# Attention and MLP on one core: where k and q of the last six quads of heads are transposed

## The chip, the core and the metric

One core of one Trainium2 chip runs the whole program. The metric is device time in microseconds (us), the median of several runs. Five engines work side by side and meet at semaphores: TensorE (PE; PEld is its weight load), VectorE (DVE), ScalarE (ACT), GpSimd (POOL) and SyncE (SP). SP and POOL also issue DMAs, each in the order of its own queue.

## The reference

Batch 8, 8 heads, 576 tokens, head depth 64, all float32. Attention with a decay by a gate f, then an MLP over the 4608 tokens by 512 features:

```
scores = q @ k.T / 8 + cum[:, None] - cum[None, :]     # cum: running sum of log f; causal
attn   = softmax(scores) @ v                           # per batch and head
x      = attn, heads side by side                      # 4608 x 512
out    = gelu_tanh(x @ w_in) @ w_out                   # 512 -> 2048 -> 512
```

## The kernel before

The work is cut twice. A **quad** is four heads of one batch: 16 quads, quad i belonging to batch i // 2. A **chunk** is 512 tokens of the MLP: 9 chunks. The MLP of a chunk runs between the quads' attention, so that TensorE always has something to do while other engines work on exponentials and sums. The MLP uses products of block sums (seven products in place of eight, L586 and L509).

The order of everything is written out by hand in tables of words (L71 to L110): FRONT, then SECOND for chunk 2, STEADY for chunks 3 to 5, FLUSH for chunk 6, LAST for chunk 7. Each word is a call (the table `ops`, L754), for example S.3.0: scores of quad 3, round 0. Numbers of quads are shifted by twice the chunk, those of chunks and batches by the chunk: S.4.0 in chunk 4 is quad 12, LB.2.0 loads values of batch 6. Every engine runs its share of the words in this order, and waits where it needs another's result.

The words around the change:

- LK, LQ (`load_one`, L206): one GpSimd DMA each loads k or q of a quad, cast to bfloat16, into k_c or q_c (two buffers each, by i % 2): head h on partitions 32h to 32h+31, 18 tokens to a partition.
- TK, TQ (`transpose_words`, L212): VectorE transposes 32x32 blocks of 4-byte words, each word two neighbouring depths in bfloat16, into kT or qT [128, tokens, 2]. Head h then has its depth on 32 partitions, as two halves c = 0, 1. kT has 64 zero tokens at either end.
- S (`scores`, L259): a quad's causal scores, in 3 rounds of 512 columns (the lists `pieces` and `rounds`). A round has, for each half c, each piece and each head, one matmul with 32 rows of depth and 128 keys; the four heads lie in four row tiles and write four PSUM banks in two tiles ps_s. Then two exponentials of ScalarE (L285), one for each pair of heads.
- M (L287): GpSimd zeroes the corners above the diagonal. VW (L227): GpSimd scales the values. D, V (L356, L374): denominators and outputs, matmuls of L347 on 32-column tiles; VectorE writes the attention's output into xT (L379). CL: a small copy.
- LB (L181): five loads of v for the batch after next, on SP's queue. Q, I, i: first layer of the MLP. T: VectorE's sums of x. G: its sums of gelus. F, f: second layer (L600), whose finished corners VectorE adds (L617 to L624) and SP stores (L625), from three buffers o_st. X, Y: ScalarE loads its table of exponentials or of gelus.

In STEADY the chunk begins with two loads (LK.4, LQ.4); LK.5 and LQ.5 follow; the four transposes TQ.3, TK.3, TK.4, TQ.4 stand in the MLP's first layer, ahead of G.0 and S.3.0. FLUSH has the last two, TK.3 and TQ.3.

Of the kernel before, what the change touches and what calls it, by code (L numbers as in the profile page):

```python
# [8 lines left out]
FP32 = mybir.dt.float32  # L9
BF16 = mybir.dt.bfloat16  # L10
AF = mybir.ActivationFunctionType
# [5 lines left out]
def kernel(  # L17
# [10 lines left out]
    nc = tc.nc  # L28

    B, H, S, D = q.shape  # L30
    BH = B * H
    NT = (S + 127) // 128
    LAST = S - 128 * (NT - 1)
    SPAD = NT * 128
    scale = 1.0 / (D ** 0.5)
# [6 lines left out]
    QPB = H // 4  # L42
# [7 lines left out]
    rounds = [(0, 512), (512, 512), (1024, 512)]  # L50
    pieces = [
        ("low", 0, 0, 64),
        (0, 64, 64, 512),
        (1, 576, 128, 448),
        (2, 1024, 256, 320),
        (3, 1344, 384, 192),
        ("high", 0, 512, 64),
    ]
    QA = 256
    split_rounds = [(1152, 384), (0, 512), (512, 320), (832, 384)]  # L60
    split_pieces = [
# [26 lines left out]
    SECOND = """  # L88
        Y F.-1.99 T.0.1 T.0.2 LB.2.0 T.0.3 T.0.4 LB.2.1 I.0.0 LB.2.2 E.0.2.2 I.0.1 LB.2.3 TK.3 LK.5 LB.2.4 E.0.2.2 TQ.3 LQ.5 TQ.4 I.0.2 E.0.2.2 I.0.3
        E.0.2.1 TK.4 G.0 VW.3 I.0.6 I.0.7 G.1.1.2 X F.0.13 S.3.0 M.3.0 f.0.9 UW.0.1 D.2 f.0.9 S.3.1 M.3.1 V.2.0 f.0.12 S.3.2 M.3.2 CL.3 V.2.1 VW.4  # L90
        f.0.14 S.4.0 UW.0.2 M.4.0 D.3 f.0.10 V.3.0 UW.0.4 CL.4 UW.0.3 S.4.1 f.0.13 M.4.1 V.3.1 S.4.2 F.0.9 M.4.2 F.0.2 F.0.1
    """

    STEADY = """
        LK.4 LQ.4 Q.0.2 Y LB.2.0 T.0.1 T.0.2 LB.2.1 F.-1.2 Q.0.2 i.0.2.4 T.0.4 LB.2.2 i.0.2.4 T.0.3 Q.0.2 TQ.3 LQ.5 Q.0.2 F.-1.6 i.0.3.4 Q.0.2 Q.0.2
        LB.2.3 TK.3 LB.2.4 LK.5 i.0.3.4 Q.0.2 TK.4 TQ.4 F.-1.99 I.0.6 i.0.7 G.0 S.3.0 X G.1.1.2 f.0.16 M.3.0 D.2 VW.3 f.0.12 S.3.1 M.3.1 V.2.0 f.0.13
        S.3.2 M.3.2 CL.3 V.2.1 VW.4 f.0.15 S.4.0 D.3 f.0.10 V.3.0 M.4.0 CL.4 S.4.1 f.0.14 M.4.1 V.3.1 S.4.2 F.0.12 M.4.2
    """

    FLUSH = """  # L100
        T.0.3 TK.3 F.-1.2 Y Q.0.2 T.0.1 T.0.2 Q.0.2 i.0.2.4 T.0.4 i.0.2.4 Q.0.2 Q.0.2 TQ.3 F.-1.6 i.0.3.4 Q.0.2 Q.0.2 i.0.3.4 Q.0.2 F.-1.99 I.0.6 i.0.7
        G.0 F.0.19 X S.3.0 G.1.1.2 D.2 f.0.11 M.3.0 f.0.4 S.3.1 M.3.1 V.2.0 VW.3 f.0.20 S.3.2 V.2.1 CL.3 M.3.2 f.0.21 f.0.12 D.3 f.0.15 V.3.0 v.3.1
    """

    LAST = """
# [6 lines left out]
    singles = ctx.enter_context(tc.tile_pool(name="singles", bufs=1))  # L112
# [4 lines left out]
    psS = ctx.enter_context(tc.tile_pool(name="psS", bufs=2, space=bass.MemoryType.PSUM))  # L117
# [3 lines left out]
    def many(n, shape, dtype, name):  # L121
        return [singles.tile(shape, dtype, name=f"{name}{i}") for i in range(n)]
# [2 lines left out]
    utri_f32 = singles.tile([128, 128], FP32, name="utri_f32")  # L125
    ones_f32 = singles.tile([128, 128], FP32, name="ones_f32")

    q_c = many(2, [128, S // 32, D], BF16, "q_c")
    k_c = many(2, [128, S // 32, D], BF16, "k_c")
    v_nat = many(2, [128, NT, H, D], FP32, "v_nat")  # L130
    qT = many(2, [128, S, 2], BF16, "qT")
    kT = many(2, [128, S + 128, 2], BF16, "kT")

    vw = many(2, [128, NT + 1, 4, D], BF16, "vw")
    pt = many(2, [128, 4, 3 * 512], BF16, "pt")
    RING = 4 * S
    xT = singles.tile([128, N_DT, RING], BF16, name="xT")
# [74 lines left out]
    def transpose_words(src, dst):  # L212
# [5 lines left out]
                .rearrange("p (a d) -> p a d", d=D // 2),  # L218
        )

    def transpose_k(i):
        return transpose_words(k_c[i % 2], kT[i % 2][:, 64:64 + S])

# [29 lines left out]
    def keep_busy(n, cols=512):  # L253

        for _ in range(n):
            nc.tensor.matmul(idle_ps[0][:, 0:cols], idle[:, 0:128], idle[:, 0:cols],
                             start=True, stop=True)

    def scores(i, r, groups=((0, 1, 2, 3),)):  # L259

        qq, p = qT[i % 2], pt[i % 2]
        if i < 2:
            off, n = split_rounds[r]
            todo = [(key, col - off, q0, nq) for (key, col, q0, nq) in split_pieces[r]]
        else:
            off, n = rounds[r]
            todo = []
            for (key, col, q0, nq) in pieces:
                a, z = max(col, off), min(col + nq, off + n)
                if a < z:  # L270
                    todo.append((key, a - off, q0 + a - col, z - a))
        for heads in groups:
            tiles = {g: psS.tile([128, 2, 512], FP32, name="ps_s", tag="s") for g in sorted({h // 2 for h in heads})}
            for c in range(2):
                for j, (key, c0, q0, nq) in enumerate(todo):
                    for h in heads:
                        nc.tensor.matmul(  # L277
                            tiles[h // 2][:, h % 2, c0:c0 + nq],
                            key_columns(i, key, h, c),
                            qq[32 * h:32 * h + 32, q0:q0 + nq, c],  # L280
                            start=(c == 0 and j == 0), stop=(c == 1),
                            skip_group_check=True,
                        )
            for g, t in tiles.items():
                nc.scalar.activation(p[:, 2 * g:2 * g + 2, off:off + n], t[:, :, 0:n], AF.Exp, scale=scale)  # L285
# [39 lines left out]
    def product(i, groups, spare, part=None):  # L325
        p = pt[i % 2]
        if part is not None:
            s0, s1 = parts[part]
            po = psM.tile([128, 512], FP32, name="po_m", tag="m")
            for (key, col, q0, nq) in sorted(sum(split_pieces[1:] if part else split_pieces[:1], []), key=lambda x: HIGH if x[0] == "high" else x[0]):  # L330
                for (r0, lhsT, h) in groups:
                    w = lhsT(HIGH if key == "high" else key)
                    nc.tensor.matmul(
                        po[r0:r0 + w.shape[-1], q0 - s0:q0 - s0 + nq], w, p[:, h, col:col + nq],
                        start=(key == 0), stop=(key == (HIGH if part else 1)),
                        skip_group_check=True,
                    )
            return po[:, 0:s1 - s0]
        if spare:
            po = psS.tile([128, 2, 512], FP32, name="ps_o", tag="s").rearrange("p a n -> p (a n)")  # L340
        else:
            po = psO.tile([128, 1024], FP32, name="po", tag="po")
        for (key, col, q0, nq) in sorted(pieces, key=lambda x: {0: 0, "low": 1}.get(x[0], 2)):
            t = {"low": LOW, "high": HIGH}.get(key, key)
            for (r0, lhsT, h) in groups:
                w = lhsT(t)
                nc.tensor.matmul(  # L347
                    po[r0:r0 + w.shape[-1], 448 + q0:448 + q0 + nq], w, p[:, h, col:col + nq],
                    start=(key in (0, "low")), stop=(key in ("low", "high")),
                    skip_group_check=True,  # L350
                )
        return po[:, 448:448 + S]

    rbs = {}

    def denominators(i, part=None):  # L356

        def column(h):

            return lambda t: (w_bf[:, i, t, h:h + 1] if t not in (0, LOW) else  # L360
                              w_bf[:, i, t, h:h + 1].to_broadcast([128, 32]))

        po = product(i, [(32 * h, column(h), h) for h in range(4)], False, part)
        n = S if part is None else parts[part][1] - parts[part][0]
        den = den_pool.tile([128, S], FP32, name="den", tag="den")
        nc.vector.transpose(out=den[:, 0:n], in_=po)
        rec = den_pool.tile([128, S // 32], FP32, name="rec", tag="rec")
        nc.vector.reciprocal(rec[:, 0:n // 32], den[:, 0:n:32])
        rb = den_pool.tile([128, S], FP32, name="rb", tag="rb")
        nc.vector.transpose(out=rb[:, 0:n].rearrange("p (c j) -> p c j", j=32),  # L370
                            in_=rec[:, 0:n // 32].unsqueeze(2).to_broadcast([128, n // 32, 32]))
        rbs[i, part] = rb[:, 0:n]

    def attn_out(i, x, spare=False, part=None):  # L374
        b, u = i // QPB, i % QPB
        po = product(i, [(32 * h, lambda t, h=h: vw[i % 2][:, t, h, x:D:2], h) for h in range(4)], spare, part)
        s0, s1 = (0, S) if part is None else parts[part]
        r0 = S * b % RING
        nc.vector.tensor_mul(xT[:, 2 * u + x, r0 + s0:r0 + s1], po, rbs[i, part])  # L379
# [371 lines left out]
    def load_values(b, half):  # L751
# [11 lines left out]
        "M": lambda i, r, *keys: mask(i, r, keys),  # L763
        "m": lambda i, r, *keys: mask_by_product(i, r, keys),
        "D": denominators,
        "V": lambda i, x, *part: attn_out(i, x, False, *part),
        "v": lambda i, x, *part: attn_out(i, x, True, *part),
        "VW": lambda i, *part: make_vw(i, nc.gpsimd, *part),
# [33 lines left out]
        "Y": load_gelu,  # L802
    }

    per_quad, per_chunk = ("S", "M", "D", "V", "v", "VW", "CL", "TK", "TQ", "LK", "LQ"), ("F", "f", "I", "i", "Q", "LB", "E", "e", "T", "t")

    def run(table, c=0):

# [15 lines left out]
    with tc.manual_schedule():  # L824
        setup()
        run(FRONT)
        for c in range(2, NCH):
            run(SECOND if c == 2 else STEADY if c < B - 2 else FLUSH if c == B - 2 else LAST if c == B - 1 else "", c)


# [28 lines left out]
```

## Time and profile before

| | |
|---|---|
| three runs | 324.68, 326.06, 326.25 us; median 326.06 |
| span of the profiled execution | 324.3 us |
| TensorE clock granted | full, in all 40 slices |
| chunk 3, 4, 5 (S.4.2 to S.4.2) | 33.6 us each: 134.0, 167.6, 201.2, 234.8 |
| score matmuls (L277) | 896, 36.3 us busy |
| VectorE's transposes of k and q (L214) | 32, mean 1.25 us |
| GpSimd's loads of k and q (L208) | 32 |

The profile shows one execution. A group's row has its line, engine, operation, shapes and count, then busy time and the mean of one in ns, then the idle time just before and what ended it. The chain of work that ended last goes back from the last instruction, at each step to what released it. Rows of stages give busy time by engine in a window, then the clock, the DMA engines' share and GB/s. TensorE's matmuls are pipelined: the distance from one group's start to the next's says more than a matmul's own length. The profile gives no time of its own for the profiled execution besides its span.

### The profile page before, as it was taken

The numbers are of one execution on the slowest core, as the hardware profiler recorded it, in microseconds if no ns is written. First come the engines' busy times: TensorE is split into PE (matmuls) and PEld (weight loads), VectorE is DVE, ScalarE is ACT, GpSimd is POOL, SyncE is SP. The second block draws the span as 40 slices with busy tenths as digits, with TensorE's granted clock in tenths as the row PEclk, the third lists the DMA queues.
The fourth block names the chain that finished last, engine by engine and source line by source line (L and its number), as shares of the span: only waits on it lengthen the run. The fifth ranks groups of instructions, "written<-read, shape, count | busy, mean of one in ns | idle before, by whom it ended". The sixth has DMA issues, their size and how long they took to land.

```text
span 324.3 us, 11816 instructions
## 1 busy us (share of the span) xinstructions
PE 310.0 (96%) x5337; PEld 221.2 (68%) x5337; DVE 241.7 (75%) x374; ACT 212.6 (66%) x242; POOL 107.0 (33%) x145
## 2 busy tenths in 40 slices
PE   0799989999999999999999999999999999999996
PEld 0557844454677667776788877767776786788785
DVE  3664307998989978779876998599885866597574
ACT  4495667686766786678667876877587743846610
POOL 8868507253111405510752056305610150000000
PEclk9999999999999999999999999999999999999999
DMA  6999999577034951395119610981001011010202
GB/s 117 232 155 165 196 250 217 139 160 143 8 67 88 227 116 36 76 213 107 36 40 211 143 40 6 206 183 35 7 32 67 17 35 53 16 50 2 99 33 98
DMA packets 47490, 33.41 MB, mean 103 GB/s; under 512 B 29776, under 2 KB 42192, under 8 KB 47440
## 3 DMA queue, kind: packets, MB, share of 16 engines
q0 software_dynamic: 9632, 15.99, 28.4%
q1 hardware_dynamic: 37664, 16.60, 18.9%
q8 instruction: 41, 0.67, 0.8%
q14 instruction: 9, 0.07, 0.1%
q10 hardware_dynamic: 144, 0.07, 0.1%
HBM read 36.85 MB, written 9.44 MB: 143 GB/s over the span
## 4 chain that ended last, share of the span: by engine, by line
PE 82%; DMA 6%; POOL 4%; ACT 4%; DVE 2%; issue 1%; POOLq 0%; DVEq 0%
PE ps_w L600 30%; PE ps_h L395 19%; PE po L347 9%; PE ps_q L520 8%; PE ps_s L277 8%; DMA w_out_sb<-in_moe_w_out_dram 4%; PE ps_u L468 4%; PE pso L667 4%; DMA q_c<-in_q_dram 2%; ACT pt L285 2%; POOL pt L291 1%; POOL w_out_sb L201 1%; POOL v_nat L185 1%; POOL w_in_sb L197 1%; PE cum_ps L721 1%
## 5 line engine op out<-in xcount | busy, mean ns | idle before, releaser
L285 ACT ACTIVATE pt<-ps_s 128x1024 bf16<-128x1024 f32 (+2 forms) x100 | 93.9, 990 | 41.3 <-PE ps_s L277 37.1
L291 POOL TENSOR_SCALAR_AFFINE_SELECT pt<-pt 128x512 bf16<-128x512 bf16 (+3 forms) x65 | 40.8, 639 | 98.0 <-ACT pt L285 75.2
L395 PE MATMUL ps_h<-xT,w_in_sb 128*128 128x512 bf16 (+1 forms) x320 | 66.8, 358 | 0.3 <-ACT gT L403 0.2
L395 PEld LDWEIGHTS <-w_in_sb 128*128 128x128 bf16 x320 | 31.2, 98 | 26.7 <-issue 0.6
L600 PEld LDWEIGHTS <-gT 128*32 128x32 bf16 (+1 forms) x1216 | 44.2, 97 | 5.5 <-issue 2.2
L403 ACT ACTIVATE gT<-ps_h 128x1024 bf16<-128x1024 f32 x34 | 34.6, 1017 | 18.7 <-PE ps_h L395 18.4
L600 PE MATMUL ps_w<-w_out_sb,gT 128*32 128x256 bf16 (+1 forms) x1008 | 42.6, 273 | 0.0
L277 PE MATMUL ps_s<-qT,kT 32*128 32x64 bf16 (+5 forms) x896 | 36.3, 263 | 4.6 <-DVE qT L214 4.3
L600 PEld LDWEIGHTS <-gsum 128*32 128x32 bf16 (+1 forms) x948 | 35.5, 97 | 3.6 <-issue 1.3
L231 POOL TENSOR_TENSOR vw<-v_nat,wT 128x1280 bf16<-128x1280 f32 (+1 forms) x13 | 29.6, 2278 | 11.8 <-DMA v_nat<-in_v_dram 11.5
L536 DVE TENSOR_TENSOR usnap<-ps_q,usnap 128x1024 f32<-128x1024 f32 x15 | 17.9, 1222 | 18.6 <-PE ps_q L520 13.2
L277 PEld LDWEIGHTS <-kT 32*128 32x128 bf16 x896 | 16.5, 93 | 20.9 <-issue 11.5
L600 PE MATMUL ps_w<-usum,gsum 128*32 128x256 bf16 (+1 forms) x791 | 29.9, 273 | 0.0
L617 DVE COPY snap<-ps_w 128x512 f32<-128x512 f32 x32 | 21.8, 681 | 6.1 <-PE ps_w L600 6.0
L531 ACT ACTIVATE gT<-usnap 128x1024 bf16<-128x1024 f32 x15 | 15.8, 1054 | 12.1 <-DVE usnap L536 11.8
L379 DVE TENSOR_TENSOR xT<-po,rb 128x576 bf16<-128x576 f32 x26 | 19.5, 752 | 5.6 <-PE po L347 5.3
L347 PE MATMUL po<-pt,vw 128*32 128x64 bf16 (+4 forms) x624 | 22.4, 278 | 0.0
L214 DVE STREAM_TRANSPOSE qT<-q_c 128x576 f32<-128x576 f32 x16 | 19.8, 1247 | 2.7 <-DMA q_c<-in_q_dram 2.5
L214 DVE STREAM_TRANSPOSE kT<-k_c 128x576 f32<-128x576 f32 x16 | 19.5, 1248 | 3.1 <-DMA k_c<-in_k_dram 3.1
L347 PEld LDWEIGHTS <-vw 128*32 128x32 bf16 x672 | 14.8, 97 | 9.3 <-issue 2.8
L208 POOL DMA_DIRECT2D k_c<-in_k_dram x16 | 9.1, 569 | 33.7 <-DVE kT L214 17.4
L520 PEld LDWEIGHTS <-w_in_sb 128*128 128x128 bf16 x160 | 15.6, 98 | 2.5 <-issue 0.4
(134 smaller groups left out, 478.4 us busy)
## 6 DMA issues: line engine op xcount, KB each, us to landing
out_dram<-o_st SPq DMA_DIRECT2D x35, 256.0 KB, 2.3
k_c<-in_k_dram POOLq DMA_DIRECT2D x16, 288.0 KB, 5.2
q_c<-in_q_dram POOLq DMA_DIRECT2D x16, 288.0 KB, 6.2
v_nat<-in_v_dram SPq DMA_DIRECT2D x16, 256.0 KB, 5.3
v_nat<-in_v_dram SPq DMA_DIRECT2D x20, 128.0 KB, 4.9
v_nat<-in_v_dram POOLq DMA_DIRECT2D x8, 256.0 KB, 8.2
w_in_sb<-in_moe_w_in_dram POOLq DMA_DIRECT2D x8, 256.0 KB, 7.6
w_out_sb<-in_moe_w_out_dram POOLq DMA_DIRECT2D x4, 512.0 KB, 11.1
```

The lines of the kernel that those rows point to most:

```text
L214: return nc.vector.transpose(out=dst.rearrange("p s c -> p (s c)").bitcast(FP32) .rearrange("p (t a) -> p a t", a=S // 32), in_=src.rearra ...
L231: return eng.tensor_mul(vw[i % 2][:, t0:t1], vb[:, t0:t1, h0:h0 + 4, :], wT[:, i, t0:t1, :].unsqueeze(3).to_broadcast([128, t1 - t0, 4, D]))
L277: nc.tensor.matmul(tiles[h // 2][:, h % 2, c0:c0 + nq], key_columns(i, key, h, c), qq[32 * h:32 * h + 32, q0:q0 + nq, c], start=(c == 0 an ...
L285: nc.scalar.activation(p[:, 2 * g:2 * g + 2, off:off + n], t[:, :, 0:n], AF.Exp, scale=scale)
L291: nc.gpsimd.affine_select(out=x, in_=x, compare_op=ALU.is_ge, fill=0.0, base=0, pattern=pattern, channel_multiplier=-1)
L347: nc.tensor.matmul(po[r0:r0 + w.shape[-1], 448 + q0:448 + q0 + nq], w, p[:, h, col:col + nq], start=(key in (0, "low")), stop=(key in ("lo ...
L379: nc.vector.tensor_mul(xT[:, 2 * u + x, r0 + s0:r0 + s1], po, rbs[i, part])
L395: nc.tensor.matmul(ph[:, j, n * cols:(n + 1) * cols], w_in_sb[:, dt, 128 * ft:128 * ft + 128], xT[:, dt, h0:h0 + cols], start=(dt == 0 and ...
L403: nc.scalar.activation(gelus(c, 2 * pr, 2), ph, AF.Gelu_apprx_tanh)
L520: nc.tensor.matmul(ps[:, k, HC * n:HC * n + HC], w[:, d, 128 * n:128 * n + 128], x[:, d, :], start=(first and n == 0 and d == 0), stop=(d ...
L600: nc.tensor.matmul(ps[c0:c0 + width, n, cols[0]:cols[1]], x[:, j, 128 * n + c0:128 * n + c0 + width], w[:, j, cols[0]:cols[1]], start=(fir ...
L617: copy(kept[name], ps)
```

## The change

From quad 10 on (`FIRST = 10`), k and q come another way.

- **LN** (`load_rows`): ten GpSimd DMAs for a batch, five of k and five of q, load 128 tokens (the last 64) of all eight heads, cast to bfloat16, token on partition, 512 columns: k_n, q_n and a shared tail. They serve two quads. They lie in the same memory as k_c and q_c.
- **DT** (`transpose_rows`): ten DMA transposes for a quad on SP's queue, each 128 tokens by 256 columns (four heads) into kT2, qT2: the same memory as kT, qT, seen as [128, 2, tokens]. A head's 64 depths lie on 64 partitions; two heads side by side, two pairs one after the other.
- **scores_by_rows**: for each pair of heads, one matmul per piece and head with 64 rows; the exponential of a pair follows its matmuls. A quad has 28 matmuls where it had 56.
- **ZK**: two small VectorE fills set the zeros that the new layout needs, once for either buffer.
- **Tables**: chunk 3 gets a table of its own, THIRD, which is the new STEADY with ZK.4 and ZK.5. In STEADY the LK, LQ, TK, TQ words go; LN.2.0 to LN.2.9 stand through the first layer, DT.4 behind X, DT.5 behind S.4.0. FLUSH loses TK.3 and TQ.3. Quad 9's transposes move from chunk 3 into SECOND (TK.5, TQ.5). `denominators` gets an argument that no table uses.

```diff
+    FIRST = 10
     SECOND = """
...
-        f.0.14 S.4.0 UW.0.2 M.4.0 D.3 f.0.10 V.3.0 UW.0.4 CL.4 UW.0.3 S.4.1 f.0.13 M.4.1 V.3.1 S.4.2 F.0.9 M.4.2 F.0.2 F.0.1
+        f.0.14 S.4.0 UW.0.2 M.4.0 D.3 f.0.10 V.3.0 UW.0.4 CL.4 UW.0.3 S.4.1 TK.5 f.0.13 M.4.1 V.3.1 S.4.2 TQ.5 F.0.9 M.4.2 F.0.2 F.0.1
+    THIRD = """
+        ZK.4 LN.2.0 LN.2.1 Q.0.2 Y LB.2.0 T.0.1 T.0.2 LN.2.2 LB.2.1 F.-1.2 Q.0.2 LN.2.3 i.0.2.4 T.0.4 LB.2.2 LN.2.4 i.0.2.4 T.0.3 LN.2.5 Q.0.2 LN.2.6 Q.0.2 F.-1.6 LN.2.7 i.0.3.4 Q.0.2 LN.2.8 Q.0.2
+        LB.2.3 LN.2.9 LB.2.4 i.0.3.4 Q.0.2 F.-1.99 I.0.6 i.0.7 G.0 S.3.0 X DT.4.0.5.1.6.2.7.3.8.4.9 G.1.1.2 f.0.16 M.3.0 D.2 VW.3 f.0.12 S.3.1 M.3.1 V.2.0 f.0.13
+        S.3.2 M.3.2 CL.3 V.2.1 VW.4 f.0.15 S.4.0 ZK.5 DT.5.0.5.1.6.2.7.3.8.4.9 D.3 f.0.10 V.3.0 M.4.0 CL.4 S.4.1 f.0.14 M.4.1 V.3.1 S.4.2 F.0.12 M.4.2
+    """
     STEADY = """
-        LK.4 LQ.4 Q.0.2 Y LB.2.0 T.0.1 T.0.2 LB.2.1 F.-1.2 Q.0.2 i.0.2.4 T.0.4 LB.2.2 i.0.2.4 T.0.3 Q.0.2 TQ.3 LQ.5 Q.0.2 F.-1.6 i.0.3.4 Q.0.2 Q.0.2
-        LB.2.3 TK.3 LB.2.4 LK.5 i.0.3.4 Q.0.2 TK.4 TQ.4 F.-1.99 I.0.6 i.0.7 G.0 S.3.0 X G.1.1.2 f.0.16 M.3.0 D.2 VW.3 f.0.12 S.3.1 M.3.1 V.2.0 f.0.13
...
-        T.0.3 TK.3 F.-1.2 Y Q.0.2 T.0.1 T.0.2 Q.0.2 i.0.2.4 T.0.4 i.0.2.4 Q.0.2 Q.0.2 TQ.3 F.-1.6 i.0.3.4 Q.0.2 Q.0.2 i.0.3.4 Q.0.2 F.-1.99 I.0.6 i.0.7
+        T.0.3 F.-1.2 Y Q.0.2 T.0.1 T.0.2 Q.0.2 i.0.2.4 T.0.4 i.0.2.4 Q.0.2 Q.0.2 F.-1.6 i.0.3.4 Q.0.2 Q.0.2 i.0.3.4 Q.0.2 F.-1.99 I.0.6 i.0.7
...
+    qk = singles.tile([128, 4 * S // 32 * D], BF16, name="qk")
...
+    k_n, q_n = (qk[:, 4 * H * D * m:4 * H * D * (m + 1)].rearrange("p (t n) -> p t n", n=H * D) for m in range(2))
+    kq_tail = qk[:, 8 * H * D:9 * H * D]
...
+    qT2 = [x.rearrange("p s c -> p (s c)").rearrange("p (g s) -> p g s", g=2) for x in qT]
+    kT2 = [x.rearrange("p s c -> p (s c)").rearrange("p (g s) -> p g s", g=2) for x in kT]
...
+    def load_rows(b, n):
+        src, t = (k, q)[n // 5], n % 5
+        p0, rows = (64 * (n // 5), S % 128) if t == NT - 1 else (0, 128)
+        dst = kq_tail if t == NT - 1 else (k_n, q_n)[n // 5][:, t]
+        return nc.gpsimd.dma_start(
+            out=dst[p0:p0 + rows].rearrange("p (h d) -> p h d", d=D),
+            in_=src[b, :, 128 * t:128 * t + rows, :].rearrange("h p d -> p h d"))
+
+    def transpose_rows(i, n):
+        t = n % 5
+        p0, rows = (64 * (n // 5), S % 128) if t == NT - 1 else (0, 128)
+        src = kq_tail if t == NT - 1 else (k_n, q_n)[n // 5][:, t]
+        c0 = 4 * D * (i % QPB)
+        dst, s0 = (qT2[i % 2], 128 * t) if n // 5 else (kT2[i % 2], 64 + 128 * t)
+        return nc.sync.dma_start_transpose(out=dst[:, :, s0:s0 + rows], in_=src[p0:p0 + rows, c0:c0 + 4 * D])
+
+    def zero_middle(i):
+        nc.vector.memset(kT2[i % 2][:, 0, 64 + S:], 0.0)
+        nc.vector.memset(kT2[i % 2][:, 1, 0:64], 0.0)
...
+    first_key = {"low": 0, 0: 64, 1: 192, 2: 320, 3: 448, "high": 64 + 512}
+
+    def scores_by_rows(i, r):
+
+        qq, kk, p = qT2[i % 2], kT2[i % 2], pt[i % 2]
+        off, n = rounds[r]
+        tiles = [psS.tile([128, 2, 512], FP32, name="ps_s", tag="s") for _ in range(2)]
+        for g, t in enumerate(tiles):
+            j = 0
+            for (key, col, q0, nq) in pieces:
+                a, z = max(col, off), min(col + nq, off + n)
+                if a >= z:
+                    continue
+                for h in range(2):
+                    nc.tensor.matmul(
+                        t[:, h, a - off:z - off],
+                        kk[64 * h:64 * h + 64, g, first_key[key]:first_key[key] + 128],
+                        qq[64 * h:64 * h + 64, g, q0 + a - col:q0 + z - col],
+                        start=(j == 0), stop=True, skip_group_check=True)
+                j += 1
+            nc.scalar.activation(p[:, 2 * g:2 * g + 2, off:off + n], t[:, :, 0:n], AF.Exp, scale=scale)
...
     def scores(i, r, groups=((0, 1, 2, 3),)):
 
+        if i >= FIRST:
+            return scores_by_rows(i, r)
...
-            run(SECOND if c == 2 else STEADY if c < B - 2 else FLUSH if c == B - 2 else LAST if c == B - 1 else "", c)
+            run(SECOND if c == 2 else THIRD if c == 3 else STEADY if c < B - 2 else FLUSH if c == B - 2 else LAST if c == B - 1 else "", c)
```

## What was predicted

> **What bounds the kernel now.** I read the page's busy shares and its chain first, then the busy time by stage, then what TensorE waited for in those stages.
>
> ```profile
> PE 310.0 (96%) x5337; PEld 221.2 (68%) x5337; DVE 241.7 (75%) x374; ACT 212.6 (66%) x242; POOL 107.0 (33%) x145
> ...
> PE 82%; DMA 6%; POOL 4%; ACT 4%; DVE 2%; issue 1%; POOLq 0%; DVEq 0%
> ```
>
> ```profile
> core 0: us, PE busy (x) PEld busy (x) DVE busy (x) ACT busy (x) POOL busy (x), PEclk, DMA share, GB/s
> 167.60:201.20 33.60, 33.60 (x733) 27.57 (x730) 27.66 (x40) 25.11 (x27) 13.00 (x16) 1.00 0.48 104
> ```
>
> ```profile
> engine line waited for: us in total, times, longest us
> PE ps_h L395 <- ACT gT L403: 0.2, 1, 0.2
> ```
>
> The second fence is chunk 4 (one pass of STEADY): 33.6 us, all of it TensorE, at full clock; VectorE (DVE) has 6 us free there and the DMA engines half the time. The third is all that TensorE waited for between 134 and 270 us, in chunks 3 to 6, which hold every step of the change. VectorE is 2% of the chain. So work taken from VectorE buys nothing by itself; only what TensorE does, or a new wait of TensorE, can move the end.
>
> **What goes from VectorE: about nothing on the path.**
>
> ```profile
> L214 DVE STREAM_TRANSPOSE qT<-q_c 128x576 f32<-128x576 f32 x16 | 19.8, 1247 | 2.7 <-DMA q_c<-in_q_dram 2.5
> L214 DVE STREAM_TRANSPOSE kT<-k_c 128x576 f32<-128x576 f32 x16 | 19.5, 1248 | 3.1 <-DMA k_c<-in_k_dram 3.1
> ```
>
> Quads 10 to 15 lose 12 transposes: 12 x 1.25 = 15 us of VectorE, all beside a full TensorE. Worth 0.
> In SECOND, quad 9's two transposes now run at about 133 to 138 us, where VectorE's timeline has no gap. V.3.1's product into xT (before: 134.52 to 135.26) then ends near 136.5, and the ps_q matmuls that read it start at 136.6 in the chain; T.0.2 ends near 138.9 with ZK.4's two small fills ahead of it, and its reader runs at 139.0 (172.59 of chunk 4 less 33.6). That is level. I put 0.2 us; bounds 0 and 1.4 (one transpose in full plus a fill).
>
> **The score matmuls: 0.9 us less.** This is chunk 4's TensorE timeline (start, length, line, form of the first, number).
>
> ```profile
> 184.26 0.70 PE L277 MATMUL ps_s<-qT,kT 32*128 32x64 bf16 x24
> 184.88 1.93 PE L600 MATMUL ps_w<-w_out_sb,gT 128*32 128x256 bf16 x64
> ...
> 188.74 0.63 PE L277 MATMUL ps_s<-qT,kT 32*128 32x64 bf16 x16
> 189.30 0.87 PE L347 MATMUL po<-pt,vw 128*32 128x512 bf16 x24
> ...
> 191.52 0.63 PE L277 MATMUL ps_s<-qT,kT 32*128 32x320 bf16 x16
> 192.08 0.87 PE L347 MATMUL po<-pt,vw 128*32 128x512 bf16 x24
> ...
> 194.52 0.69 PE L277 MATMUL ps_s<-qT,kT 32*128 32x64 bf16 x24
> ```
>
> From start to the next line's start a round takes 0.62, 0.56 and 0.56 us: 1.74 a quad. Columns: four 32-row matmuls run side by side, so round 0 streams 2 x (64+448+64) = 1152 columns, rounds 1 and 2 stream 2 x 512 = 1024. A column costs 0.67 us / 1600 = 0.42 ns by the 24 matmuls of L347 (0.68 us in the chain, 1600 columns four wide). That makes 0.48, 0.43 and 0.43 us, and leaves 0.14, 0.13 and 0.13 us a round. The new rounds have half the matmuls (28 a quad, not 56), two side by side with 64 rows, once for each pair of heads where there were two halves of the depth: 1152, 1024, 1024 columns again. The streaming stays; only the 0.13 us can change. It is the same for 24 and for 16 matmuls, so it is not a price per instruction, and I take most of it as the price of going from one tiling to the other and back, which the new form pays too. Value: 0.05 us a round less, as half as many starts must be staggered; bounds 0.13 less and 0.08 more (pairs that hide the next weights less well). 6 quads x 3 rounds x 0.05 = 0.9 us; bounds -2.4 and +1.4.
> The Trainium skill, TensorEngine Tiling (Array Packing), Key Properties under Tiling Modes, says that changing the tiling mode drains the engine. By that rule alone all of the 0.13 us stays and this term is 0 in place of 0.9.
> The first pair's tile is whole after half a round, so ScalarE starts some 0.28 us sooner. In FLUSH that can take away TensorE's one stall in these chunks (0.2 us, behind ScalarE): -0.2.
>
> **The new loads: hidden.** Chunks 3 to 5 get 10 GpSimd loads each in place of 4. The nearest row is v_nat's load on GpSimd, with the same pieces: 0.87 us of issue, 8.2 us to landing.
>
> ```profile
> k_c<-in_k_dram POOLq DMA_DIRECT2D x16, 288.0 KB, 5.2
> ...
> v_nat<-in_v_dram POOLq DMA_DIRECT2D x8, 256.0 KB, 8.2
> ...
> out_dram<-o_st SPq DMA_DIRECT2D x35, 256.0 KB, 2.3
> ```
>
> GpSimd is free from 170.9 (after M.4.2) to 188.7 in chunk 4 but for three issues: 10 x 0.87 = 8.7 us end at 179.6; the last load lands at 187.8, by the longest v_nat landing (13.6 us) at 193.2. M.3.0 and VW.3, next in GpSimd's queue, are not delayed. The bytes read are the same 2.36 MB a chunk, so the DMA share stays near 0.5 plus the transposes.
>
> **The transposes: hidden, with some 4 us to spare.** Quad 12's ten stand on SP's queue behind the last store of the chunk's output.
>
> ```profile
> 181.45 1.24 DVE L214 STREAM_TRANSPOSE qT<-q_c 128x576 f32<-128x576 f32 x1
> 182.53 0.68 DVE L622 COPY o_st<-ps_w 128x512 f32<-128x512 f32 x1
> ```
>
> The L622 copy runs after VectorE's transposes; without them it follows its matmuls (done 180.7), so SP is free at about 181.6. The reader is S.4.0 at 194.5: 12.9 us. The trace has no DMA transpose. For SP's issue the rows are 0.38 us (a store) and 0.77 us (a v load: five in 3.79 us). For the moving of 64 KB, the hardware queue's mean packet is 26 ns (18.9% of 16 x 324.3 us over 37664): 64 packets of 1 KB make 0.1 us over 16 engines, 256 of 256 B 0.4 us, 2048 of 32 B 3.3 us. I take 0.6 us each, set by issue, as the source rows are 512 B and the results 256 B a partition: 181.6 + 6.0 + 2.3 for the last landing = 189.9; with the last load at 187.8, two more transposes and a landing: 191.3. Both are ahead of 194.5. Break-even: 10t + 2.3 = 12.9, t = 1.06 us. Quad 13's ten follow one store (its copy is over at 191.6) and are read at 217.8; next chunk's loads wait for them, and they are done by 201, before 204.6. Stores queued behind transposes have three buffers and wait up to 12 us already.
> If the cover goes, each us of lateness is one us of TensorE in each of three chunks.
>
> **Sum.** -0.9 - 0.2 + 0.2 = -0.9 us on a span of 324.3: 323.4. The three runs have a median of 326.06, 1.76 above that span; I carry the difference over: **325.1 us**.
>
> **Rivals.**
> *Pairs without the round's overhead (faster).* All 0.13 us of 18 rounds goes, and FLUSH's stall: -2.4 - 0.2 + 0.2 = 323.7. For it: half the weight loads and starts. Against it: the overhead doesn't follow the number of matmuls. Chance 0.18.
> *Transposes or loads a little late (slower).* At t = 1.3 us quad 12's end is 181.6 + 13 + 2.3 = 196.9, 2.4 us late, and the following chunks lose up to as much; loads at 1.5 times the longest landing (20.4 us) give 179.6 + 20.4 + 3.5 = 203.5, 9 us late. That is 327 to 338, say 330. It decides from t = 1.06, or from a last landing at 191. For it: 204 to 222 GB/s and a full DMA share at 171 to 179. Chance 0.23.
> *Transposes one after another (slower).* If SP takes the store's whole landing, 2.3 us, for each: the first quad is 12.4 us late, and a chunk's SP queue holds 20 x 2.3 + 5.4 us (five v loads, four stores) = 51.4 against 33.6, twice more 17.8: +48, 373 us. It sets in at t = (33.6 - 5.4) / 20 = 1.41. Chance 0.10.
> The Trainium skill, VectorE: DVE Perf Modes, The three transpose paths, gives 1309 ns for a 128x128 transpose by DMA and 311 ns by VectorE: two of them a transpose here, 2.6 us, would be that rival and beyond. The skill's Advanced Engine Details and Errata, X-Bar Transpose, calls them as fast as plain DMAs, which would be the forecast. No row here decides between them.
> *Not what it says:* transposed element by element, 32768 packets x 26 ns / 16 = 53 us each, thousands of us in all. Chance 0.02.
>
> **Chances and range.** 0.5% (1.6 us) is about what a measurement of this kernel can tell from no change. The forecast's case has 0.47 (323.8 to 327), nearly all within 0.5%, 0.07 of it faster, 0.03 slower; the faster rival 0.18. So faster 0.25, same 0.37, slower 0.38. The range runs from 323.0 to 338.0: below it lies 0.05 (more than the overhead gone), above it about 0.13.
>
> **What would show it.** Right: TensorE's waits between 134 and 270 us still near 0.2 us; rounds at 0.57, 0.51, 0.51; SP's transposes of a quad in under 10 us. Wrong: a wait of the score matmuls for a transpose at S.4.0 or S.3.0, GpSimd's masks starting late behind loads, a gap at 136.5 us, or rounds over 0.62 us.

## The result, and the profile after

The changed kernel takes **348.31 us** (median of 4 runs, 345.99 to 350.95); the kernel before, beside it, 325.6 us (4 runs). The ratio is 1.071 (95% interval 1.064 to 1.078). The forecast was 325.1 us with a range up to 338.0: the time lies 10 us above the range. The profiled execution of the changed kernel has a span of 348.3 us, 24.0 more than before. Medians here and below are of the fast runs; one slower run each of e5 (352.73 us) and e8 (336.88 us) is given beside them.

The page of the changed kernel, its busy shares and its chain:

```profile
PE 316.6 (91%) x5153; PEld 224.2 (64%) x5169; DVE 229.5 (66%) x366; ACT 212.7 (61%) x242; POOL 126.2 (36%) x163
...
PE 70%; DMA 10%; POOL 6%; SPq 5%; issue 4%; ACT 2%; DVE 1%; POOLq 0%; DVEq 0%
```

VectorE is 12 us less busy, as meant, and TensorE has fewer matmuls. But TensorE's share of the chain fell from 82% to 70%; DMA, SP's queue and "issue" took its place. TensorE's busy time even rose by 6.6 us, with 168 matmuls fewer (by the weight loads, 5337 and 5169; the records of 16 more matmuls are missing).

Chunk 4 as a stage (columns as in the prediction's second fence):

```profile
171.47:216.25 44.78, 36.35 (x681) 28.79 (x674) 23.74 (x36) 25.11 (x27) 19.02 (x23) 0.92 0.84 105
```

The chunk takes 44.8 us in place of 33.6. TensorE is busy for 36.4 of them, at a mean clock of 0.92, and the DMA engines are busy for 0.84 of the time in place of 0.48, though the GB/s are the same. Chunks 3 and 5 take 40.0 and 42.1 us: together 26.1 us more than before, and all that happens ahead of chunk 3 and behind chunk 5 is level within 2 us.

What TensorE waited for between 100 and 300 us:

```profile
engine line waited for: us in total, times, longest us
PE ps_s L305 <- DMA qT<-qk: 11.7, 5, 4.5
PE ps_w L656 <- issue: 4.0, 2, 2.3
PE ps_s L333 <- issue: 2.2, 1, 2.2
...
```

Two rows of 0.2 us are left out. L305 is the new score matmuls. They wait 11.7 us for transposes: that is the stall that the prediction named as its refutation. The two "issue" rows, 6.2 us, are stalls in which the profile shows nothing that TensorE waited for; no step of the prediction had them. The TensorE timeline of chunk 4 shows both kinds:

```profile
188.71 0.67 PE L305 MATMUL ps_s<-qT,kT 64*128 64x64 bf16 x12
189.31 1.93 PE L656 MATMUL ps_w<-w_out_sb,gT 128*32 128x256 bf16 x64
...
194.83 1.05 PE L656 MATMUL ps_w<-usum,gsum 128*32 128x256 bf16 x32
197.59 0.29 PE L656 MATMUL ps_w<-usum,gsum 128*32 128x256 bf16 x4 [1.71 <-issue]
...
200.80 0.20 PE L305 MATMUL ps_s<-qT,kT 64*128 64x64 bf16 x2
205.54 0.36 PE L305 MATMUL ps_s<-qT,kT 64*128 64x448 bf16 x2 [4.54 <-DMA qT<-qk]
208.08 0.72 PE L305 MATMUL ps_s<-qT,kT 64*128 64x64 bf16 x8 [2.17 <-DMA qT<-qk]
208.72 1.53 PE L403 MATMUL po<-pt,w_bf 128*32 128x512 bf16 x24
```

S.4.0 starts at 200.8, and its operands come piece by piece until 208. The first two lines give a round: 0.60 us from start to start, where it was 0.62.

SP's queue in the same chunk (start, time on SP, operation):

```profile
188.66 1.13 SPq L681 DMA_DIRECT2D out_dram<-o_st  x1
189.91 1.77 SPq L247 DMA_TRANSPOSE kT<-qk  x1
...
193.07 3.51 SPq L247 DMA_TRANSPOSE kT<-qk  x1
...
204.39 1.19 SPq L247 DMA_TRANSPOSE kT<-qk  x1
205.67 1.19 SPq L247 DMA_TRANSPOSE qT<-qk  x1
```

Ten transposes run from 189.91 to 206.86: 17 us in place of the 6 that I had put. The last two move the tails of 64 rows; they cost 1.19 us like those of 128. All 60 of them:

```profile
L247 SPq DMA_TRANSPOSE kT<-qk x30: 1182/1200/3514, 146.8 to 262.4; - x30
L247 SPq DMA_TRANSPOSE qT<-qk x30: 1167/1236/2732, 148.1 to 263.7; - x30
...
DMA to landing us min/median/max: 2.3/3.3/8.3
```

1.2 us is floor and median at once (ns: least, median, most).

The waits of 17.9 us are not the whole loss. The rest is TensorE's clock. The profile's records of the granted clock show half speed from 165.3 to 168.7, 206.2 to 213.0, 243.8 to 247.2 and 250.6 to 254.0 us, each behind a stall. One of these stretches as a stage:

```profile
204.00:214.00 10.00, 6.29 (x110) 3.68 (x114) 2.89 (x5) 2.06 (x3) 1.07 (x2) 0.66 0.28 67
```

24 matmuls of L403 take 1.5 us here (208.72 on the timeline above), 0.87 at full clock.

### The profile page after: what moved, and what is told of

The parts are those of the page before. It is cut to its first block, busy times and chain, and to the rows that moved or that the text cites. A ratio compares the mean times of both kernels' runs of the same rounds, so it can differ in the third digit from the quotient of the medians.

```text
span 348.3 us, 11597 instructions
## 1 busy us (share of the span) xinstructions
PE 316.6 (91%) x5153; PEld 224.2 (64%) x5169; DVE 229.5 (66%) x366; ACT 212.7 (61%) x242; POOL 126.2 (36%) x163
## 4 chain that ended last, share of the span: by engine, by line
PE 70%; DMA 10%; POOL 6%; SPq 5%; issue 4%; ACT 2%; DVE 1%; POOLq 0%; DVEq 0%
PE ps_w L656 25%; PE ps_h L451 16%; PE po L403 8%; PE ps_q L576 7%; SPq L247 5%; DMA qk<-in_q_dram 4%; DMA w_out_sb<-in_moe_w_out_dram 4%; PE ps_u L524 4%; PE pso L723 3%; PE ps_s L333 3%; PE ps_s L305 3%; DMA qT<-qk 2%; ACT pt L341 2%; POOL qk L237 1%; POOL pt L347 1%
## 5 line engine op out<-in xcount | busy, mean ns | idle before, releaser
L341 ACT ACTIVATE pt<-ps_s 128x1024 bf16<-128x1024 f32 (+2 forms) x64 | 59.0, 973 | 25.7 <-PE ps_s L333 22.4
L451 PE MATMUL ps_h<-xT,w_in_sb 128*128 128x512 bf16 (+1 forms) x307 | 65.6, 357 | 0.9 <-issue 0.2
L311 ACT ACTIVATE pt<-ps_s 128x1024 bf16<-128x1024 f32 x36 | 34.9, 1021 | 38.7 <-PE ps_s L305 38.6
L459 ACT ACTIVATE gT<-ps_h 128x1024 bf16<-128x1024 f32 x34 | 34.6, 1017 | 18.9 <-PE ps_h L451 18.6
L656 PE MATMUL ps_w<-w_out_sb,gT 128*32 128x256 bf16 (+1 forms) x1008 | 44.9, 285 | 0.0
L656 PE MATMUL ps_w<-usum,gsum 128*32 128x256 bf16 (+1 forms) x791 | 31.6, 281 | 4.0 <-issue 4.0
L263 POOL TENSOR_TENSOR vw<-v_nat,wT 128x1280 bf16<-128x1280 f32 (+1 forms) x13 | 29.6, 2277 | 12.0 <-DMA v_nat<-in_v_dram 11.7
L592 DVE TENSOR_TENSOR usnap<-ps_q,usnap 128x1024 f32<-128x1024 f32 x15 | 17.9, 1221 | 18.3 <-PE ps_q L576 13.0
L333 PE MATMUL ps_s<-qT,kT 32*128 32x64 bf16 (+5 forms) x560 | 24.7, 264 | 5.0 <-DVE qT L226 2.6
L435 DVE TENSOR_TENSOR xT<-po,rb 128x576 bf16<-128x576 f32 x26 | 19.6, 753 | 12.8 <-PE po L403 12.5
L422 DVE STREAM_TRANSPOSE den<-po 128x576 f32<-128x576 f32 x14 | 10.9, 781 | 20.8 <-PE po L403 20.7
L403 PE MATMUL po<-pt,vw 128*32 128x64 bf16 (+4 forms) x624 | 24.2, 293 | 0.0
L305 PE MATMUL ps_s<-qT,kT 64*128 64x64 bf16 (+3 forms) x168 | 12.8, 269 | 11.7 <-DMA qT<-qk 11.7
L333 PEld LDWEIGHTS <-kT 32*128 32x128 bf16 x560 | 11.4, 93 | 16.6 <-issue 10.3
L403 PEld LDWEIGHTS <-vw 128*32 128x32 bf16 x672 | 15.3, 101 | 10.6 <-issue 4.2
```

The lines of the kernel that those rows point to most:

```text
L263: return eng.tensor_mul(vw[i % 2][:, t0:t1], vb[:, t0:t1, h0:h0 + 4, :], wT[:, i, t0:t1, :].unsqueeze(3).to_broadcast([128, t1 - t0, 4, D]))
L305: nc.tensor.matmul(t[:, h, a - off:z - off], kk[64 * h:64 * h + 64, g, first_key[key]:first_key[key] + 128], qq[64 * h:64 * h + 64, g, q0 ...
L333: nc.tensor.matmul(tiles[h // 2][:, h % 2, c0:c0 + nq], key_columns(i, key, h, c), qq[32 * h:32 * h + 32, q0:q0 + nq, c], start=(c == 0 an ...
L403: nc.tensor.matmul(po[r0:r0 + w.shape[-1], 448 + q0:448 + q0 + nq], w, p[:, h, col:col + nq], start=(key in (0, "low")), stop=(key in ("lo ...
L451: nc.tensor.matmul(ph[:, j, n * cols:(n + 1) * cols], w_in_sb[:, dt, 128 * ft:128 * ft + 128], xT[:, dt, h0:h0 + cols], start=(dt == 0 and ...
L459: nc.scalar.activation(gelus(c, 2 * pr, 2), ph, AF.Gelu_apprx_tanh)
```

## The experiments

"Before" is timed beside each kernel: 324.8, 324.6, 324.5 and 324.5 us in the four series. The edits change the words of THIRD and STEADY alone, unless another place is shown.

**e1: no transposes.** Scores of quads 10 to 15 are then of what lies in kT and qT.

```diff
-  DT.4.0.5.1.6.2.7.3.8.4.9
-  DT.5.0.5.1.6.2.7.3.8.4.9
```

> Leaves out all 60 DMA transposes; loads by rows and pair matmuls stay (the scores of quads 10 to 15 are made from whatever kT and qT hold). Theory A (SP spends 1.2 us or more on every transpose, and ten of them don't fit ahead of S.4.0): no TensorE wait is left, 33.5 us a chunk, 324 to 326 us. Theory B (the row loads, slow in 128-byte packets, are what costs): the late masks or late issue stay, over 335 us. Theory C (TensorE's unexplained stalls near 154, 196 and 241 us come from the loads' traffic alone): those stalls of 2 us stay, with their clock drops: 332 to 336 us.

Measured: 324.28 us, ratio 1.000 (0.997 to 1.003), full clock, no wait of TensorE over 0.2 us. So everything lost needs the transposes. The row loads by themselves, all 30, cost nothing.

**e2: no row loads**; the transposes move stale rows.

```diff
-  LN.2.0 ... LN.2.9   (each where it stood)
```

> Leaves out the 30 row loads; the 60 transposes stay and move old data. Theory A: the transposes still take 1.2 us each on SP, so quad 10 ends some 12.4 us after SP reaches them, S.4.0 waits 0 to 2 us in chunk 3; if the excess of 3 to 4 us a quad (single transposes of 2 to 3.5 us) is due to the loads' traffic beside them, it goes, and the time is 326 to 334 us. If the excess belongs to the transposes alone: 340 to 348 us. Theory B: 325 us, with no wait at S.4.0.

Measured: 341.4 us, ratio 1.052 (1.048 to 1.056). A transpose takes 1.23 us on SP as in the change (the median), ten of them 14 to 16 us, and TensorE still waits:

```profile
PE ps_s L305 <- DMA qT<-qk: 9.2, 6, 2.2
```

There is no "issue" stall any more. So the price of a transpose isn't made by the row loads, but the stalls without a cause in the profile need them.

**e3: score pairs only**, neither row loads nor transposes (scores of stale columns).

```diff
-  LN.2.0 ... LN.2.9
-  DT.4.0.5.1.6.2.7.3.8.4.9
-  DT.5.0.5.1.6.2.7.3.8.4.9
```

> Leaves out row loads and transposes both; what stays of the change is the pair matmuls and VectorE without its 12 transposes. All theories: TensorE full, rounds of 0.60, 0.54 and 0.54 us in place of 0.62, 0.56 and 0.56, so 18 x 0.02 = 0.4 us less than before and perhaps 0.2 us in FLUSH: 325.0 us against 325.6. This is the most that the idea could bring. If VectorE's 15 us had been worth something on the path it would show here as 1 us or more.

Measured: 324.38 us, ratio 0.999 (0.997 to 1.001), span 322.9, full clock. This is the most that the idea can bring if all its DMAs are free: nothing that can be measured. VectorE's transposes were worth 0, as forecast.

**e4: half the transposes**: five of ten for each quad, three of k and two of q (the rest of the columns stale).

```diff
-  DT.4.0.5.1.6.2.7.3.8.4.9
+  DT.4.0.5.1.6.2
-  DT.5.0.5.1.6.2.7.3.8.4.9
+  DT.5.0.5.1.6.2
```

> Every quad's ten transposes cut to five (n = 0, 5, 1, 6, 2; the other tokens keep old data); loads stay. Theory A: SP is done after 5 x 1.24 = 6.2 us and some excess, long before S.4.0: no wait for a transpose there; 325 to 327 us, or 331 to 334 if the stalls near 154, 196, 241 us stay with half the transposes. Theory B: over 335 us, as the loads are the same.

Measured: 325.55 us, ratio 1.003 (1.001 to 1.005), full clock, no wait over 0.2 us. A transpose takes 1.2 us here too. Half of them cost 0.8 us, all of them 23: the loss has a threshold, as a queue that runs past its due time has.

**e5: half the width**: each transpose moves 128 columns in place of 256 (one pair of heads; the other pair's columns are stale).

```diff
-        return nc.sync.dma_start_transpose(out=dst[:, :, s0:s0 + rows], in_=src[p0:p0 + rows, c0:c0 + 4 * D])
+        return nc.sync.dma_start_transpose(out=dst[:, 0, s0:s0 + rows], in_=src[p0:p0 + rows, c0:c0 + 2 * D])
```

> The same 60 transposes, each of 128 columns in place of 256 (the second pair of heads of a quad keeps old data). Theory A1 (a fixed 1.2 us of SP per transpose instruction): still 1.2 us each, S.4.0 waits as before, 340 to 349 us. Theory A2 (SP's time goes by the number of 128-column blocks or of 256-byte packets): 0.6 us each, ten in 6 to 8 us, no wait at S.4.0, 325 to 327 us.

Measured: 346.25 us (a second run took 352.73): no gain that can be told. Half the bytes cost the same time on SP (the profile is of the second run):

```profile
L247 SPq DMA_TRANSPOSE kT<-qk x30: 1106/1182/2437, 148.5 to 264.7; - x30
```

In these runs the price is one of the instruction, for 64 or 128 rows, 128 or 256 columns alike.

**e6: the first ten earlier**, right behind the chunk's last v load and ahead of its stores.

```diff
-  X DT.4.0.5.1.6.2.7.3.8.4.9 G.1.1.2
+  X G.1.1.2
-  LB.2.4 i.0.3.4
+  LB.2.4 DT.4.0.1.2.3.4.5.6.7.8.9 i.0.3.4
```

> Only moved: quad 2c+4's ten transposes stand behind the last v load in SP's queue, ahead of the store of F.-1.99, k's five first. Theory A: they start some 4 us sooner and end about 2 us ahead of S.4.0, so chunk 3 loses nothing at S.4.0; but SP's queue holds some 25 us of transposes, 5 of their excess, 2 of stores and 4 to 8 of v loads in a chunk of 33.6, so chunks 4 and 5 are each 2 to 6 us long: 328 to 338 us. If only the place mattered and not the sum of the queue: 325 to 327 us. The 2 us stalls of TensorE (loads and transposes beside instruction fetches) may stay: 6 us more on either.

Measured: 340.97 us, ratio 1.051 (1.043 to 1.058). The wait for transposes is 8.2 us in place of 11.7, "issue" 4.9 us. In chunk 4 they start 0.3 us behind S.3.0 (186.15 to 185.84), in the change 1.2 us behind it: little is won, because SP's queue is full up to there with the second ten of the chunk before, stores and v loads, and the ten themselves take 18.9 us. In chunk 3 they do start 3.8 us sooner, and S.4.0 still waits 1.2 us, where I had expected no loss. The time lies in the expected band only with the 6 us that I had allowed for the "issue" stalls. SP is still what is late.

**e7: as e6, and the five v loads of a chunk on GpSimd's queue**, behind the row loads.

```diff
-  LB.2.0 ... LB.2.4
-  LN.2.9
+  LN.2.9 LG.2.0 LG.2.1 LG.2.2 LG.2.3 LG.2.4
+        "LG": lambda b, t: load_v(b, ts=(t,), eng=nc.gpsimd) if b < B else [],
```

> As e6, and the v loads of chunks 3 to 5 are issued by GpSimd behind the row loads (its table of words gets one that loads v from GpSimd). SP's queue then holds 25 + 5 + 2 = 32 us in a chunk of 33.6. Theory A: no lasting wait for transposes: 325 to 329 us, and 3 to 9 us less than e6. If SP's queue isn't what bounds it: the same as e6.

Measured: 345.61 us, ratio 1.064 (1.058 to 1.070), so my expectation was missed. The wait for transposes is gone altogether, and the time is no better than in e6, because the other stalls grew to 14.5 us (6.2 in the change):

```profile
PE ps_w L656 <- issue: 8.8, 2, 5.0
PE ps_s L333 <- issue: 5.7, 1, 5.7
```

So the lateness of transposes is only half of the matter. The three stalls stand behind matmuls number 2398, 3164 and 3802 of the program, in e6 as in e7, though at other times (154, 198 and 239 us here). Between them lie 766 and 638 matmuls; with a weight load each that is 1532 and 1276 instructions, 5.98 and 4.98 times 256. The page's instruction queue moves packets of 16384 bytes, 40 of them (packets, MB, share of 16 engines):

```profile
q8 instruction: 40, 0.66, 0.8%
```

For 5169 matmuls and as many weight loads that is 63 bytes each, so about 256 instructions to a block of 16384 bytes. TensorE stopped where a block of instructions ends. The DMA records of the trace show the block behind it coming late:

```
                      last GpSimd load packet   block of instructions   TensorE
                      before the stall ends     starts to move          goes on
after       chunk 3         153.0 us                152.6 us             155.7 us
            chunk 4         193.9                   193.7                197.6
            chunk 5         239.4                   239.7                242.9
e7          chunk 3         158.1*                  157.4                160.1
            chunk 4         200.2                   200.7                203.4
            chunk 5         240.1                   240.0                243.4
* two more packets, at 158.8 and 159.2
```

In these six stalls the block starts within 0.7 us of the moment at which GpSimd's loads have drained (but for those two packets), and TensorE goes on 2.7 to 3.9 us after the block has started. Other traces are less strict: late blocks of e6, e8 and e11 start 0.5 to 4.2 us ahead of the last packet, and then take 1.4 to 4.6 us to move, against 0.9 to 1.8 in the kernel before. The next experiments test whether such late blocks are what stops TensorE.

**e8: as e7, with fewer instructions**: the fills f (four tiles of 32 columns) become F (128 columns wide), the same products in a quarter of the matmuls.

```diff
-  f.0.16 f.0.12 f.0.13 f.0.15 f.0.10 f.0.14   (each where it stood)
+  F.0.16 F.0.12 F.0.13 F.0.15 F.0.10 F.0.14
```

> As e7 (first ten transposes earlier, v loads on GpSimd), and in chunks 3 to 5 the fills f.0.n of the output product become F.0.n: 128 columns wide instead of four tiles of 32, a quarter as many matmuls and weight loads for the same products. Theory A, TensorE ran out of instructions: its 'issue' stalls in e7 (5.7, 5.0, 3.8 us) stand at the ends of blocks of about 256 instructions, whose successor comes by the same DMA engines and came late; with fewer instructions a block lasts longer, so the stalls go or shrink to under 4 us in all, and the time is 324 to 331 us. Theory B, the stalls are not the supply of instructions but something that transposes do to TensorE's reads or semaphores: the stalls stay at 11 us or more, 341 to 347 us. In both, no wait of the score matmuls for a transpose.

Measured: 332.78 us (330.17, 332.78 and 334.28; a fourth run took 336.88), ratio 1.025 (1.017 to 1.032). In the profiled run, the fastest of the four, the stalls are 0.6 us in place of 14.5 and the wait for transposes 0.4, with every DMA of e7 in place:

```profile
PE po L403 <- issue: 0.6, 1, 0.6
PE ps_s L305 <- DMA qT<-qk: 0.4, 1, 0.4
```

The blocks still come late: three of them start at 156.1, 193.0 and 226.9 us, the same three (counted in order) in the control e9 at 150.4, 189.2 and 221.6. With 720 matmuls fewer, and as many weight loads (35 blocks in all, not 40), TensorE still has instructions when they do. Less the 2.9 us that the wider fills cost by themselves (e9), the median is 329.9 us: inside the band of theory A, far from that of theory B. Over e9 itself 5.5 us remain in the median and 3.1 between the profiled spans; no profile shows the waits of the slower runs.

**e9: wider fills alone**: the control, as e3 with F for f.

> As e3 (score pairs only, no row loads, no transposes, quads 10 to 15 scored from stale columns), with the wider fills of e8: the control of e8, what the wider fills cost or bring by themselves. Both theories: e3's 324.4 us within 2 us, no issue stall over 0.5 us. If it is slower by d, d is taken off e8's time before the theories are told apart.

Measured: 327.28 us, ratio 1.009 (1.006 to 1.012), no stall over 0.2 us. The wide fills by themselves cost 2.9 us against e3, 0.9 us beyond the band.

**e10: as e7, without row loads** (transposes of stale rows).

```diff
-  LN.2.0 ... LN.2.9
```

> As e7, without the row loads of chunks 3 to 5 (the transposes move stale rows, so the scores of quads 10 to 15 are of old data): ten transposes of the first quad with a clear queue ahead of them, v loads on GpSimd. Theory A1, the instruction blocks come late only when transposes and the row loads' 27648 packets of 128 bytes are in flight together: no issue stall over 0.5 us, no wait for transposes over 2 us, 324 to 329 us. Theory A2, the transposes alone (with the v loads) hold the blocks up: stalls of 8 us or more stay, 338 to 346 us.

Measured: 324.4 us, ratio 0.999 (0.997 to 1.002), no wait of TensorE over 0.2 us, clock 0.998. All 60 transposes run, at their full price:

```profile
L247 SPq DMA_TRANSPOSE kT<-qk x30: 1179/1219/2404, 140.0 to 236.0; - x30
```

So transposes of 1.2 us can be hidden whole if SP reaches the first ten 6.8 us sooner (140.0 in place of 146.8) and has no v loads to issue; once they are in time, they harm TensorE only with the row loads beside them. GpSimd's loads end at 142.6, 176.6 and 210.1 us here, and the blocks that came late in e7 start at 149.4, 185.0 and 218.3, with no load in flight. Theory A1 holds; against e7 the one edit is worth 21 us.

**e11: TensorE kept busy in the gap**: matmuls that compute nothing ahead of S.4.0.

```diff
+    def keep_scores_busy(n):
+        t = psS.tile([128, 2, 512], FP32, name="ps_i", tag="s")
+        for _ in range(n):
+            nc.tensor.matmul(t[:, 0, :], idle[:, 0:128], idle, start=True, stop=True)
-  S.4.0
+  KB.10 S.4.0   (THIRD; KB.20 in STEADY)
```

> The change as it is, with matmuls that compute nothing ahead of S.4.0: 10 of 512 columns in chunk 3 (2.1 us at full clock), 20 in chunks 4 and 5 (4.3 us each). Theory A, some 8 of the 24 us are the half clock that is granted after TensorE stood idle: the wait for transposes falls from 11.7 to 1 to 6 us, the half-clock stretches at 165 to 169, 206 to 213 and 250 to 254 us shorten, and the time falls to 338 to 345 us although work was added. Theory B, the half clock is no consequence of the gaps or is made up for later: the time stays or grows, 347 to 353 us.

Measured: 346.02 us (344.08 to 347.15), ratio 1.066 (1.060 to 1.071): between the two bands, 2.3 us under the change's median (the runs of the two overlap) with 10.7 us of matmuls added (50 x 512 columns x 0.42 ns). The stage that ran at 0.66 above:

```profile
204.00:214.00 10.00, 10.00 (x221) 6.93 (x219) 6.06 (x11) 5.66 (x6) 1.71 (x3) 1.00 0.25 45
```

The clock is full there, and twice as many matmuls fit in. No wait for transposes is left, and the mean clock is 0.989 in place of 0.976: 4.6 us of the span by (1 - clock) x span. "Issue" stalls grew by 1.2 us. So the half clock does follow the gaps. Two half-clock stretches are left, at 197.4 and 238.4 us, each behind a stall at a block's end (2.6 and 3.5 us): that is where the time fell by less than I had put.

**e12: as e7, row loads in long pieces**: the same bytes and issues, 128 stretches of 2048 bytes a load in place of 1024 of 256 (other numbers than the rows, so the scores are of wrong data).

```diff
-            out=dst[p0:p0 + rows].rearrange("p (h d) -> p h d", d=D),
-            in_=src[b, :, 128 * t:128 * t + rows, :].rearrange("h p d -> p h d"))
+            out=dst[p0:p0 + rows],
+            in_=src[b, 0:4].rearrange("h (p a) d -> (h p) (a d)", p=32)[0:rows, 128 * t:128 * t + H * D])
```

> As e7, but each row load reads 128 stretches of 2048 bytes (and writes 1024 bytes to a partition) in place of 1024 pieces of 256 bytes (128 written): the same bytes, issues and places in the queue, an eighth of the packets. It takes other numbers than the rows of q and k, so the scores of quads 10 to 15 are of wrong data. Theory P, the blocks of instructions wait behind the row loads' many packets (27648 of 32 ns are 55 us of 16 engines): 'issue' stalls under 2 us in all in place of 14.5, clock at 0.99 or more, 324 to 331 us. Theory B, what counts is that GpSimd's loads are in flight beside the transposes, whatever their pieces: stalls of 8 us or more stay, 338 to 346 us.

Measured: 341.15 us, ratio 1.053 (1.049 to 1.056).

```profile
PE ps_w L656 <- issue: 5.2, 2, 3.5
PE ps_s L333 <- issue: 3.6, 1, 3.6
```

8.8 us of stalls in place of 14.5. My theory P, that the many packets do it, falls: theory B has the time and the stalls. The number of packets seems to make it worse (the median is 4.5 us under e7's), but loads of GpSimd in long pieces hold the blocks up as well. Again the late blocks start (155.4, 196.5, 233.5 us) 0.5 to 0.7 us after the loads' last packets (154.9, 196.0, 232.8).

**The sum of the loss**, from each profiled execution. The last two columns should agree; e3's span, 322.9, is the base, 324.9 (e9) for e8.

| | wait for transposes | "issue" stalls | (1 - clock) x span | matmuls added | sum | span over base |
|---|---|---|---|---|---|---|
| after | 11.7 | 6.2 | 8.4 | 0 | 26.3 | 25.4 |
| e2 | 9.2 | 0 | 5.1 | 0 | 14.3 | 15.9 |
| e6 | 8.2 | 4.9 | 3.4 | 0 | 16.5 | 17.7 |
| e7 | 0 | 14.5 | 8.6 | 0 | 23.1 | 22.1 |
| e8 | 0.4 | 0.6 | 1.0 | 0 | 2.0 | 3.1 |
| e10 | 0 | 0 | 0.6 | 0 | 0.6 | -1.3 |
| e11 | 0 | 7.4 | 3.8 | 10.7 | 21.9 | 21.9 |
| e12 | 0 | 8.8 | 3.7 | 0 | 12.5 | 13.6 |

They agree within 2 us. None of the kernels beats the one before: e3 and e10, in which the cost is gone, are level with it.

## Why the prediction failed, step by step

- **VectorE's transposes: 0.** Right: e3 has none of them for these quads and is level with before.
- **SECOND's moved transposes: 0.2 us.** Right: no gap over 0.2 us at the moved place.
- **Score rounds: 0.05 us less each.** The sign was right, the size too large: 0.60, 0.54 and 0.54 us in place of 0.62, 0.56, 0.56, so 0.02 each, 0.4 us for 18 rounds; most of the 0.13 us stayed. FLUSH's stall (0.25 us, at 242.6 us before) is gone in e3 and in the change, as forecast.
- **The row loads: hidden.** Right for their own readers: the issue ended at 185.2 in chunk 4 (forecast 179.6; the chunk began 4.5 us late; GpSimd had four issues there before, not three, on which nothing rests), the masks were on time, and e1 is level. Wrong on the DMA engines: for the same bytes GpSimd's loads take them for 18.5 us of chunk 4 in place of 6.9, so the DMA share did not stay at 0.5 plus the transposes. Wrong beyond that, too: beside the transposes they delay TensorE's instructions. I looked for their readers and for GpSimd's queue, and not for other users of the DMA engines.
- **"I take 0.6 us each, set by issue": the step that failed first.** A transpose took 1.2 us of SP at least, 1.45 on average over all 60, and 1.7 from start to start in chunk 4's first ten. My own break-even was 1.06 us. I had rows of a store (0.38) and a v load (0.77) and took the middle; the experiments show a price that neither rows nor columns change. Beside this the Trainium skill, VectorE: DVE Perf Modes, The three transpose paths, gives 1309 ns for 128x128 by DMA: near what one instruction took, but I had doubled it for 256 columns, and e5 shows that width costs nothing. The Trainium skill, Advanced Engine Details and Errata, X-Bar Transpose, calls such transfers as fast as plain ones; here SP spends 1.2 us at least on one, and 0.38 on a plain store in the kernel before (0.37 to 1.7 in the change).
- **SP is free at 181.6.** With the chunk's delay of 4.5 us that is 186.1; it was 189.9. Two v loads (3.25 us from 185.3) stood ahead, since they had queued behind the ten transposes before. So 10.9 us were left until S.4.0 began, not 12.9. The plain issues had grown, too: a v load takes SP 1.42 us on average in the change, 0.74 before, 0.75 in e1 and 0.82 in e2, so this as well needs both kinds of DMA.
- **The rival "one after another".** Its condition came true and its price did not. It sets in at 1.41 us a transpose, and the mean was 1.45: SP issued from 163.6 to 206.9 us with no gap over 0.2 us. But it reckoned with 2.3 us each, and with 373 us.
- **"each us of lateness is one us of TensorE": the step that failed next.** The rival "a little late" had this mechanism and a fit price (at 1.3 us a transpose, 2.4 us late a chunk), and its 330 us was still 18 too low. e2, which has the lateness alone, shows its size: 9.2 us of waits and a span 15.9 us longer, the rest mostly the clock. The stalls at block ends, 6.2 us and their part of the clock, were in no rival.

What stays open: why a block of instructions comes late until GpSimd's loads have drained or nearly so, and only when transposes are in flight. In e1 blocks start in the midst of the same loads (181.3 us, loads until 186.2) without harm. The runs show that both kinds of DMA are needed, and that neither long pieces nor v loads taken off SP's queue mend it; they do not show which part of the DMA engines or rings holds it. Nor is it shown that both kinds are enough: in e4 they are in flight together for some 3 us a chunk (5 to 6 in the change) and no stall follows, but the block that falls there starts 0.4 us after the first transpose is issued (180.6 us, loads until 183.2).

## What to carry to other kernels

Price a DMA transpose of this size by the instruction, not by its bytes, and add up the whole queue that it stands in, with the loads and stores that will queue behind it in the next round: that sum, against the time of the reader, decides, and it decides as a threshold. On a kernel that TensorE bounds, new DMA traffic is not free because its own readers are on time: look for stalls at the same matmul numbers with no releaser, which here were late instructions, and reckon that a gap of TensorE can cost more than its length through the clock (in e2 9.2 us of waits went with 15.9 us of span). Where the unit that is relieved has next to no share of the chain, do the half of the change that costs nothing first (here e3): it shows in one run that there was nothing to gain.

## What the runs showed of the hardware

- **The clock follows the gaps by windows.** The half-clock stretches last 3.41 or 6.83 us, and within each trace they begin whole multiples of 3.41 us apart. In the changed kernel a window of 3.41 us at full clock in which TensorE stood still for 2.16 to 3.05 us was followed by half clock (four windows, ending at 165.3, 206.2, 243.8 and 250.6 us); 1.50, 1.62 and 1.80 us left the clock full. The 1.50 us belong to a gap of 2.19 us at 153.5, which the end of a window (155.0, counted back from 165.3) cuts in two. The other traces put the line near 1.8 us, as far as the modelled ends of matmuls tell: 2.08 us in e11 and 1.83 in e2 brought half clock, 1.77 in e6 and 1.85 in e5 did not. At half clock less was enough to stay there: 1.86 us here (206.2 to 209.6), 1.25 in e7. The Trainium skill, TensorE: Matmul & The Clock Gate, Part 1, has the two speeds and free-running windows of 3413 ns, and half clock after at least one idle window: the trace agrees on the length, and shows that a window need not be idle in full.
- **Small packets are dear.** The row loads' 27648 packets of 128 bytes took 32 ns each by the DMA records, in e1 (without transposes) as in the change; those of 2304 bytes of the old loads took 219 ns: 0.25 against 0.10 ns a byte. Chunk 4 moves 4.7 MB in place of 3.5, the rest being the transposes, and the DMA share goes from 0.48 to 0.84 though the chunk is 11 us longer.
- **TensorE's instructions come by DMA in blocks of 16384 bytes**, 0.9 to 1.8 us each in the kernel before, and up to 2.5 us at the stalls of the changed kernel. Many small matmuls use them up faster: with a quarter of the fills' matmuls the stalls under the same traffic fell from 14.5 to 0.6 us (e7 and e8, one profile each).
